# Five weight pieces instead of three converted inside the last attention steps of a decay attention followed by two MLPs

## The chip, the cores and the metric

The kernel runs on one core of a Trainium2 chip. The metric is the device time of one execution in microseconds (us). The engines of the core are TensorE (PE in the rows, with its weight loads as PEld), VectorE (DVE), ScalarE (ACT), GpSimd (POOL) and SyncE (SP, which here only issues DMAs). Each engine takes its instructions strictly in the order in which the program gives them to it, and waits at an instruction until its inputs and its output buffer are ready.

## The reference, cut to what matters

```python
# decay attention, 2 batches x 8 heads, 768 positions, head size 64, blocks of 64
for b in range(nb):
    intra = einsum('bhic,bhjc->bhij', qb, kb) * Dmask          # scores inside a block
    intra = einsum('bhij,bhjd->bhid', intra, vb)
    inter = einsum('bhid,bhde->bhie', qb * lam_pow, kv_state)  # what earlier blocks left
    out[:, :, sl] = intra + inter
    kv_state = lam_block * kv_state + einsum('bhsd,bhse->bhde', kb * rev_pow, vb)
x = out as (1536 tokens, 512)
h = x @ w_in;  x = (h * cos(h)) @ w_out         # first MLP, d_ff = 2048
h = x @ w_in2; x = (h * sigmoid(h)) @ w_out2    # second MLP, d_ff = 2048
```

The weights arrive as 64-bit floats.

## The kernel before

**Attention.** The loop over `c` from 0 to `UP` = 6 treats 128 positions (two blocks) a step, and is skewed: step `c` transposes k and q of chunk `c` on TensorE (`att_k`, `att_q`: PSUM tile `pt`, copied out by ScalarE as `kT` and `qT`, L203 and L209; `pt` has one buffer), and finishes chunk `c-1`: `att_kv` (PSUM tile `pkv`, L241), `att_state` (DVE adds it to the decayed state, L254, and POOL decays the sum, L260), `att_scores` (PSUM tile `psc`, L270, multiplied by the decay table on DVE into `at`, L274), `att_inter` (state times q, PSUM tile `pso`, L293), `att_intra` (v times `at`, added into `pso`, L308) and `att_x`. `att_x` writes the chunk of x in two float32r parts: `xhi` on ScalarE (L317) and the rest `xlo` on DVE (L318). Chunk `c` is written (c) below: `xhi`(5) is the last `xhi` of the attention.

**Weights.** A *piece* (j, p) is one tile of 128 of d_ff: p = 0 its columns of `w_in`, p = 1 its rows of `w_out`; 32 tiles make 64 pieces. `load_w` fetches a piece of 512 KB as raw 64-bit words from SyncE's queue (three buffers). `rebias_w`/`convert_w` make float32 of it: ScalarE L93, DVE L104 (`sb`) and DVE L105 (`w`). `split_w` makes two float32r parts: `hi` on ScalarE (L115) and `lo` on POOL (L116). As each piece is converted, the next load is issued (`load_next`).

**MLPs.** A second loop over `t` (96 of them) computes a tile of d_ff for 512 tokens a step: `gemm_in(t)` (12 matmuls of 128x128 by 512 into PSUM tile `h`, L347, which has two buffers; w `hi` by `xhi`, w `lo` by `xhi`, w `hi` by `xlo`, four each), the activation (ScalarE L362 and L371, DVE L363 and L377, ScalarE L379, POOL L385) and, two steps later, `gemm_out(t - 2)` (12 matmuls into `y`, L403). `h(t+1)` takes the PSUM buffer that `h(t-1)` leaves when DVE has read it at L377. h(t), y(t) and n(t) are written for these tiles of step t. Steps 0 to 3 use d_ff tiles 0 to 3, and the next eight steps the same four tiles for the other tokens; tile 4 is first wanted at t = 12.

The order is written out by hand. `first` lists the pieces converted inside the attention loop, `plan` the pieces converted at each step t of the MLP loop, and the loads go in the same order.

Of the kernel before, what the change touches and what calls it, by code (L numbers as in the profile page):

```python
# [21 lines left out]
UP = 6  # L22
# [5 lines left out]
def tile_decay_attention__two_mlps(  # L28
# [46 lines left out]
    def load_w(j, piece):  # L75
        L, f = divmod(j, FT)
        r = stage.tile([P, TB, 2], U32, tag="raw", name="raw")
        if piece == 0:
            nc.sync.dma_start(
                out=r.rearrange("p (k f) t -> p k (f t)", k=KT), in_=w_in[L][:, :, 2 * f * P:2 * (f + 1) * P]  # L80
            )
        else:
            nc.sync.dma_start(out=r.rearrange("p c t -> p (c t)"), in_=w_out[L][f * P:(f + 1) * P, :])
        raw[j, piece] = r
# [70 lines left out]
    def tables():  # L155

        step = stage.tile([P, 2, B, NP, C], F32, tag="raw", name="step")
        by_s = lamb.rearrange("p (s y) -> p y s", y=2)
        for r in range(2):
            for b in range(B):  # L160
                nc.vector.tensor_copy(step[:, r, b], by_s[:, r ^ b, :, None].to_broadcast([P, NP, C]))
        nc.vector.memset(step[:, :, :, :, 0:1], 0.0)
        scan(*(t.rearrange("p r b s i -> p (r b s i)") for t in (dm, step, diag)))
        nc.gpsimd.tensor_copy(rev, dm[:, :, :, :, C - 1].rearrange("p r b s -> p b s r"))

        first = stage.tile([P, B, NP, C], F32, tag="raw", name="first")
        nc.gpsimd.memset(first, 0.0)
        for y in range(2):
            for b in range(B):
                nc.gpsimd.tensor_copy(first[half[y], b, :, 0], by_s[half[y], y ^ b])  # L170
        for y in range(2):
            scan(*(t[half[y]].rearrange("p b s i -> p (b s i)") for t in (qp, step[:, y], first)))
# [3 lines left out]
    def load_qkv(c, parts="kqv", engine=None):  # L176
        r = slice(c * P, (c + 1) * P)
        for part in parts:
            t = ap_2.tile([P, B, H, D], F32, tag=part, name=part, bufs=3 if part == "v" else 2)
            src = [{"q": q, "k": k, "v": v}[part][b, :, r, :].rearrange("h p d -> p h d") for b in range(B)]  # L180
            eng = engine or nc.sync
            if part == "v":
                for b in range(B):
                    eng.dma_start(out=t[:, b], in_=src[b])
            else:
                eng.dma_start(out=t[:, 0], in_=src[0])
                for y in range(2):
                    eng.dma_start(out=t[:, 1, y::2, :], in_=src[1][:, 1 - y::2, :])
            qkv[c, part] = t
# [10 lines left out]
    def att_k(c, pool, tag):  # L200
        pt = transposed(c, "k", pool, tag)
        kT = ap_2.tile([P, B, NP, P], F32, tag="kT", name="kT")
        nc.scalar.copy(kT, pt)  # L203
        tr[c, "k"] = kT
# [29 lines left out]
    def att_kv(c, pool, tag):  # L234
        ps = pool.tile([P, 2, B, NP, D], F32, tag=tag, name="pkv")
        kt, vt = kd.pop(c), qkv[c, "v"]
        for b in range(B):
            for s in range(NP):
                for r in range(2):
                    for n in range(2):  # L240
                        nc.tensor.matmul(  # L241
                            ps[half[r], n, b, s, :], kt[half[n], b, 2 * s + r, :], vt[half[n], b, 2 * s + (b ^ r), :],
                            start=True, stop=True,
                        )
        pkv[c] = ps
# [185 lines left out]
    def evacuate_lo():  # L431
        if lows:
            yl, y, yh = lows.pop(0)
            nc.gpsimd.tensor_tensor(out=yl, in0=y, in1=yh, op=ALU.subtract)


    first = [(0, 0), (1, 0), (0, 1)]
    plan = {0: [(2, 0)], 1: [(1, 1), (3, 0)], 2: [(2, 1)], 3: [(3, 1)]}
    for slot, tiles in ((4, range(4, 15)), (27, range(15, 19)), (43, range(19, 27)), (67, range(27, 32))):
        for j in tiles:  # L440
            for p in range(2):
                plan[slot + 2 * (j - tiles[0]) + p] = [(j, p)]
    queue = first + [x for t in sorted(plan) for x in plan[t]]

    with tc.manual_schedule():
        nc.scalar.dma_start(out=lamb, in_=lam.partition_broadcast(P))
        load_qkv(0, "k")
        load_qkv(0, "q", nc.scalar)
        load_qkv(0, "v")
        load_qkv(1)  # L450
        zeros = stage.tile([P, TB], mybir.dt.bfloat16, tag="raw", name="zeros")
        nc.vector.memset(zeros, 0.0)
        cold = ps_o.tile([P, B, TB], F32, tag="o", name="cold")

        for _ in range(WARM):
            nc.tensor.matmul(cold[:, 0, :], zeros[:, 0:P], zeros, start=True, stop=True)
        nc.vector.memset(half_pi, math.pi / 2.0)

        nc.scalar.activation(quarter, half_pi, AF.Sin)
        nc.vector.memset(quarter, 0.25)  # L460
        nc.gpsimd.memset(ident, 0.0)
        nc.gpsimd.affine_select(
            out=ident, in_=ident, compare_op=ALU.not_equal, fill=1.0, base=0, pattern=[[-1, P]], channel_multiplier=1
        )

        diag = stage.tile([P, 2, B, NP, C], F32, tag="raw", name="diag")
        for n in range(2):
            nc.gpsimd.tensor_copy(
                diag[half[n]].rearrange("p r b s i -> p (r b s) i"), ident[half[n], None, half[n]].to_broadcast([C, B * H, C])
            )  # L470
        tables()
        loaded = 0

        def load_next():
            nonlocal loaded
            if loaded < len(queue):
                load_w(*queue[loaded])
                loaded += 1


        for c in range(UP + 1):
            if c < UP:
                att_k(c, ps_t, "t")
            if c > 0:
                att_kv(c - 1, ps_kv, "kv")
                att_state(c - 1, 0)
            if c < UP:
                att_kdec(c)
                if c + 2 < SC:
                    load_qkv(c + 2, "k")  # L490
                att_q(c, ps_t, "t")
                if c + 2 < SC:
                    load_qkv(c + 2, "qv")
            if c > 0:
                att_scores(c - 1, ps_s, "s")
                att_inter(c - 1, ps_o, "o")
            if c < UP:
                att_qdec(c)
            if c > 0:
                att_state(c - 1, 1)  # L500
                att_intra(c - 1)
                att_x(c - 1)
            if UP - 3 <= c < UP:
                load_next()
            for piece in {UP - 1: first[:1], UP: first[1:]}.get(c, ()):
                convert_w(piece)
                load_next()
                split_w(piece)
        psum_up.close()
        if UP == SC:  # L510
            att_pools.close()
        ps_h = ctx.enter_context(tc.tile_pool(name="ps_h", bufs=2, space=PSUM))
        ps_y = ctx.enter_context(tc.tile_pool(name="ps_y", bufs=6, space=PSUM))

        gpool = ctx.enter_context(tc.tile_pool(name="gpool", bufs=3))
        tpool = ctx.enter_context(tc.tile_pool(name="tpool", bufs=2))
        parts = ctx.enter_context(tc.tile_pool(name="parts", bufs=NB))
        wextra = ctx.enter_context(tc.tile_pool(name="wextra", bufs=TILES - EARLY))
        for t in range(N + 1):
            if t < N and t not in ph:  # L520
                gemm_in(t)
            if 1 <= t < N + 1:
                act_g(t - 1)
                act_glo(t - 1)
            new = t > 2 and t - 2 in starts
            if new:
                evacuate(starts[t - 2] - 1)
            evacuate_lo()
            pieces = plan.get(t, [])
            for piece in pieces:  # L530
                convert_w(piece)
                load_next()
            if t < N:
                act_a(t)
                act_b(t)
            for piece in pieces:
                split_w(piece)
            for piece in plan.get(t + 1, [])[:1]:
                rebias_w(piece)
            if new and t + 1 < N:  # L540
                gemm_in(t + 1)
            if 2 <= t < N:
                gemm_out(t - 2)

        for m in range(4):
            gemm_out(N - 2, (m,))
            gemm_out(N - 1, (m,))
        evacuate(len(runs) - 1)
# [30 lines left out]
```

## Time and profile before

| | |
|---|---|
| median of three executions | 609.42 us (608.39 to 610.33) |
| the profiled execution | 610.34 us, of which its span, first to last instruction, is 607.6 us |
| TensorE busy | 575.1 us, 95% of the span |
| VectorE, ScalarE, GpSimd busy | 323.8, 256.9, 259.3 us |
| attention ends (`xhi`(5) starts) | 73.16 us after the span's start |

Times in rows are counted from the span's start. The profiled execution lies 0.9 us above the median of the others, inside their scatter at its upper edge.

### The profile page before, as it was taken

The page shows a single profiled execution, that of the slowest core. Times are in us where ns is not written, and L with a number is a line of the kernel's source. Part 1 is how long each engine was busy: PE and PEld are TensorE (multiplying, and loading weights), DVE is VectorE, ACT ScalarE, POOL GpSimd, SP SyncE. Part 2 cuts the span into 40 slices and gives each one's busy share as a digit, 9 for nine tenths or more (in the row PEclk, how much of TensorE's full clock was granted, in tenths as well). Part 3 has the DMA queues.
Part 4 walks back from the last instruction along what each step waited for, and adds up shares of the span by engine and source line. Part 5 has one row for each costly group of instructions (what it writes and reads, how often), then busy time and mean ns, then how long its engine had stood idle before and what let it go on. Part 6 is the DMA issues. An engine that isn't in the chain of part 4 may idle for free.

```text
span 607.6 us, 9554 instructions
## 1 busy us (share of the span) xinstructions
PE 575.1 (95%) x3912; PEld 472.8 (78%) x3912; DVE 323.8 (53%) x349; ACT 256.9 (42%) x425; POOL 259.3 (43%) x201
## 2 busy tenths in 40 slices
PE   5866779999999999999999999999999999999997
PEld 2755657888888888888888888888888888888885
DVE  4354578888788877862257876611246721201212
ACT  2223355665755554563365643422433532212220
POOL 5432346555545444553266575532245541222210
PEclk9999989999999999999999999999999999999999
DMA  9986153332333322320022333300033100100101
GB/s 176 196 178 185 39 173 105 104 104 74 101 104 105 104 70 73 101 70 2 0 71 69 105 104 105 102 4 1 0 105 98 41 0 2 69 1 0 70 0 70
DMA packets 61051, 46.75 MB, mean 77 GB/s; under 512 B 38992, under 2 KB 55376, under 8 KB 61008
## 3 DMA queue, kind: packets, MB, share of 16 engines
q1 hardware_dynamic: 58768, 45.62, 26.4%
q10 hardware_dynamic: 2240, 0.53, 0.5%
q8 instruction: 30, 0.49, 0.3%
q14 instruction: 13, 0.11, 0.1%
HBM read 43.00 MB, written 3.15 MB: 76 GB/s over the span
## 4 chain that ended last, share of the span: by engine, by line
PE 91%; issue 4%; DVE 2%; ACT 1%; DMA 1%; POOL 0%; SPq 0%; DVEq 0%; ACTq 0%; POOLq 0%
PE y L403 43%; PE h L347 42%; PE pt L195 2%; PE pso L308 1%; PE pkv L241 1%; DMA k<-in_k_dram 1%; PE psc L270 1%; PE pso L293 1%; DVE w L105 1%; POOL lo L116 0%; ACT kT L203 0%; ACT xhi L317 0%; DVE sb L104 0%; ACT w L93 0%; DVE at L274 0%
## 5 line engine op out<-in xcount | busy, mean ns | idle before, releaser
L385 POOL TENSOR_TENSOR gl<-s,gh 128x512 fp32r<-128x512 f32 x95 | 133.8, 1408 | 139.1 <-ACT gh L379 124.4
L377 DVE TENSOR_TENSOR s<-h,s 128x512 f32<-128x512 f32 x96 | 66.4, 692 | 197.2 <-ACT s L373 159.2
L116 POOL TENSOR_TENSOR lo<-w,hi 128x512 fp32r<-128x512 f32 x64 | 83.5, 1305 | 156.7 <-ACT hi L115 156.7
L347 PE MATMUL h<-xhi,hi 128*128 128x512 f32 x384 | 103.5, 391 | 4.2 <-DVE s L377 3.2
L347 PE MATMUL h<-xhi,lo 128*128 128x512 f32 x384 | 103.8, 392 | 0.9 <-POOL lo L116 0.9
L347 PE MATMUL h<-xlo,hi 128*128 128x512 f32 x384 | 103.2, 391 | 0.0
L105 DVE SCALAR_TENSOR_TENSOR w<-w,sb 128x512 uint32<-128x512 uint32 x64 | 93.0, 1454 | 8.3 <-ACT w L93 1.9
L373 ACT ACTIVATE s<-h 128x512 f32<-128x512 f32 x48 | 28.8, 599 | 141.9 <-PE h L347 141.9
L347 PEld LDWEIGHTS h<-xhi,hi 128*128 128x128 f32 x384 | 71.7, 188 | 20.3 <-ACT hi L115 4.3
L347 PEld LDWEIGHTS h<-xhi,lo 128*128 128x128 f32 x384 | 72.3, 189 | 17.0 <-POOL lo L116 2.1
L347 PEld LDWEIGHTS h<-xlo,hi 128*128 128x128 f32 x384 | 72.6, 189 | 15.3
L104 DVE TENSOR_SCALAR sb<-raw 128x512 uint32<-128x512 uint32 x64 | 81.4, 1273 | 0.1
L403 PE MATMUL y<-gh,hi 128*128 128x512 f32 x192 | 74.7, 389 | 0.0
L403 PE MATMUL y<-gl,hi 128*128 128x512 f32 x192 | 74.7, 389 | 0.0
L403 PE MATMUL y<-hi,gl 128*128 128x512 f32 x192 | 74.7, 389 | 0.0
L403 PE MATMUL y<-lo,gh 128*128 128x512 f32 x192 | 74.7, 389 | 0.0
L403 PE MATMUL y<-hi,gh 128*128 128x512 f32 x192 | 74.7, 389 | 0.0
L403 PE MATMUL y<-gh,lo 128*128 128x512 f32 x192 | 74.7, 389 | 0.0
L379 ACT CAST gh<-s 128x512 fp32r<-128x512 f32 x96 | 58.9, 613 | 31.6 <-DVE s L377 23.6
L371 ACT ACTIVATE s<-s,consts 128x512 f32<-128x512 f32 x48 | 34.8, 724 | 65.4 <-DVE s L363 65.4
L362 ACT ACTIVATE n<-h,consts 128x512 int32<-128x512 f32 x48 | 33.0, 687 | 41.5 <-PE h L347 41.5
L363 DVE SCALAR_TENSOR_TENSOR s<-h,n 128x512 f32<-128x512 f32 x48 | 32.9, 685 | 31.4 <-ACT n L362 30.2
(57 smaller groups left out, 535.2 us busy)
## 6 DMA issues: line engine op xcount, KB each, us to landing
raw<-in_moe_w_in_dram SPq DMA_DIRECT2D x32, 512.0 KB, 3.8
raw<-in_moe_w_out_dram SPq DMA_DIRECT2D x32, 512.0 KB, 3.3
v<-in_v_dram SPq DMA_DIRECT2D x12, 256.0 KB, 5.0
out_dram<-part SPq DMA_DIRECT2D x12, 256.0 KB, 2.1
k<-in_k_dram SPq DMA_DIRECT2D x6, 256.0 KB, 5.2
k<-in_k_dram SPq DMA_DIRECT2D x12, 128.0 KB, 4.4
q<-in_q_dram SPq DMA_DIRECT2D x5, 256.0 KB, 4.5
q<-in_q_dram SPq DMA_DIRECT2D x10, 128.0 KB, 4.6
```

The lines of the kernel that those rows point to most:

```text
L104: nc.vector.tensor_scalar(out=sb, in0=r[:, :, 0], scalar1=2.0**-29, scalar2=7.0, op0=ALU.mult, op1=ALU.min)
L105: nc.vector.scalar_tensor_tensor(out=w, in0=w, scalar=3, in1=sb, op0=ALU.logical_shift_left, op1=ALU.bitwise_or)
L116: nc.gpsimd.tensor_tensor(out=lo, in0=w, in1=hi.bitcast(F32), op=ALU.subtract)
L347: nc.tensor.matmul(h, w[:, kt * P:(kt + 1) * P], x[:, kt, :], start=(n == 0 and kt == 0), stop=(n == 2 and kt == KT - 1),)
L362: nc.scalar.activation(n, h, AF.Identity, scale=1.0 / (2.0 * math.pi), bias=quarter)
L363: nc.vector.scalar_tensor_tensor(out=s, in0=h, scalar=1.0 / (2.0 * math.pi), in1=n, op0=ALU.mult, op1=ALU.subtract)
L371: nc.scalar.activation(s, s, AF.Sin, scale=2.0 * math.pi, bias=half_pi)
L373: nc.scalar.activation(s, ph[t], AF.Sigmoid)
L377: nc.vector.tensor_tensor(out=s, in0=ph.pop(t), in1=s, op=ALU.mult)
L379: nc.scalar.copy(gh, s)
L385: engine.tensor_tensor(out=gl, in0=act.pop(t), in1=gt[t][0].bitcast(F32), op=ALU.subtract)
L403: nc.tensor.matmul(y[m], w, x, start=(i == 0 and n == 0), stop=(i == n_tiles - 1 and n == 2))
```

## The change

Three lines of numbers change. The attention loop converts five pieces, one at the end of step c = 4, two at the end of c = 5 and two at the end of c = 6, in place of none, one and two. The MLP loop's `plan` has at t = 0, 1, 2 one piece each, and the pieces of tiles 4 to 14 start at t = 3 in place of 4. The sequence of pieces and of loads stays the same.

```diff
-    first = [(0, 0), (1, 0), (0, 1)]
-    plan = {0: [(2, 0)], 1: [(1, 1), (3, 0)], 2: [(2, 1)], 3: [(3, 1)]}
-    for slot, tiles in ((4, range(4, 15)), (27, range(15, 19)), (43, range(19, 27)), (67, range(27, 32))):
+    first = [(0, 0), (1, 0), (0, 1), (2, 0), (1, 1)]
+    plan = {0: [(3, 0)], 1: [(2, 1)], 2: [(3, 1)]}
+    for slot, tiles in ((3, range(4, 15)), (27, range(15, 19)), (43, range(19, 27)), (67, range(27, 32))):
...
-            for piece in {UP - 1: first[:1], UP: first[1:]}.get(c, ()):
+            for piece in {UP - 2: first[:1], UP - 1: first[1:3], UP: first[3:]}.get(c, ()):
                 convert_w(piece)
                 load_next()
                 split_w(piece)
```

Two places in the engines' orders matter below. The first is ScalarE between the end of step c = 4 and the end of c = 5. Before, `kT`(5) stands right behind `xhi`(3) (`xhi_722<-pso_824`):

```order
L317 CAST xhi_722<-pso_824 128x2x4x128
L203 COPY kT_910<-pt_901 128x1024
L209 COPY qT_960<-pt_951 128x1024
L317 CAST xhi_1070<-pso_997 128x2x4x128
L93 ACTIVATE w_1076<-raw_726 128x512
L115 CAST hi_1083<-w_1076 128x512
```

Now the two ScalarE instructions of piece (0, 0) stand between them:

```order
L317 CAST xhi_722<-pso_824 128x2x4x128
L93 ACTIVATE w_901<-raw_726 128x512
L115 CAST hi_908<-w_901 128x512
L203 COPY kT_921<-pt_912 128x1024
L209 COPY qT_971<-pt_962 128x1024
L317 CAST xhi_1081<-pso_1008 128x2x4x128
```

So `kT`(5) has moved behind a whole conversion, of which `hi` itself waits for DVE. The second place is DVE between `xlo`(4) at the end of c = 5 and `xlo`(5) at the end of c = 6. Before, one conversion (`sb`, `w`) stands ahead of the last state and the last `at`:

```order
L318 TENSOR_TENSOR xlo_1071<-pso_997,xhi_1070 128x2x4x128
L104 TENSOR_SCALAR sb_1078<-raw_726 128x512
L105 SCALAR_TENSOR_TENSOR w_1076<-w_1076,sb_1078 128x512
L254 TENSOR_TENSOR state_1120<-pkv_1087,sdec_1034 128x512
L274 TENSOR_TENSOR at_1155<-psc_1122,dm_91 128x1024
L318 TENSOR_TENSOR xlo_1071<-pso_1157,xhi_1070 128x2x4x128
```

Now two stand there, those of pieces (1, 0) and (0, 1):

```order
L318 TENSOR_TENSOR xlo_1082<-pso_1008,xhi_1081 128x2x4x128
L104 TENSOR_SCALAR sb_1089<-raw_899 128x512
L105 SCALAR_TENSOR_TENSOR w_1087<-w_1087,sb_1089 128x512
L104 TENSOR_SCALAR sb_1100<-raw_906 128x512
L105 SCALAR_TENSOR_TENSOR w_1098<-w_1098,sb_1100 128x512
L254 TENSOR_TENSOR state_1142<-pkv_1109,sdec_1045 128x512
L274 TENSOR_TENSOR at_1177<-psc_1144,dm_91 128x1024
L318 TENSOR_TENSOR xlo_1082<-pso_1179,xhi_1081 128x2x4x128
```

The state and `at` of chunk 5 have moved behind a second conversion. Behind `xlo`(5), the first activation's n(0) (L362 on ScalarE) has three pieces' L93 ahead of it before and after the change: (1, 0), (0, 1) and (2, 0) then, (2, 0), (1, 1) and (3, 0) now. TensorE's order does not change at all.

## Rows read from the trace of the kernel before

**Rows 1.** The page's first line.

```profile
span 607.6 us, 9554 instructions
```

**Rows 2.** Windows, one core: stretch; busy us (instructions) by engine; PEclk; DMA; GB/s.

```profile
95.00:200.00 105.00, 105.00 (x464) 86.69 (x464) 86.82 (x88) 63.69 (x111) 54.24 (x40) 1.00 0.31 96
```

**Rows 3.** Timeline: start us, us, engine, line, operation, [idle before <-releaser]; first MLP steps.

```profile
83.09 0.69 DVE L377 TENSOR_TENSOR s<-h,s 128x512 f32<-128x512 f32 x1 [0.79 <-ACT s L371]
...
83.93 1.40 PE L347 MATMUL h<-xhi,hi 128*128 128x512 f32 x4 [3.18 <-DVE s L377]
...
88.36 0.40 PE L403 MATMUL y<-gl,hi 128*128 128x512 f32 x1
...
91.11 1.07 PE L347 MATMUL h<-xhi,hi 128*128 128x512 f32 x4
...
92.88 1.20 PE L347 MATMUL h<-xhi,lo 128*128 128x512 f32 x4 [0.69 <-POOL lo L116]
```

**Rows 4.** Windows around h(2), columns as in Rows 2.

```profile
80.80:84.00 3.20, 0.07 (x1) 0.10 (x1) 2.41 (x4) 1.79 (x4) 0.71 (x2) 1.00 0.57 191
84.00:88.40 4.40, 4.40 (x13) 3.28 (x14) 4.16 (x5) 1.78 (x4) 2.35 (x2) 0.61 0.38 119
```

**Rows 5.** Timeline, end of step c = 4 to end of c = 5.

```profile
56.71 1.01 ACT L317 CAST xhi<-pso 128x1024 fp32r<-128x1024 f32 x1 [4.94 <-PE pso L308]
...
57.77 1.01 ACT L203 COPY kT<-pt 128x1024 f32<-128x1024 f32 x1
...
60.08 1.09 PE L195 MATMUL pt<-ident,q 128*128 128x128 f32 x8
...
62.34 1.22 DVE L274 TENSOR_TENSOR at<-psc,dm 128x1024 f32<-128x1024 f32 x1 [1.38 <-PE psc L270]
...
63.80 1.50 PE L308 MATMUL pso<-at,v 64*64 64x64 f32 x64
...
65.35 1.01 ACT L317 CAST xhi<-pso 128x1024 fp32r<-128x1024 f32 x1 [3.07 <-PE pso L308]
```

**Rows 6.** Timeline, end of c = 5 to end of c = 6.

```profile
67.54 0.42 DVE L104 TENSOR_SCALAR sb<-raw 128x512 uint32<-128x512 uint32 x1
...
68.67 0.68 DVE L254 TENSOR_TENSOR state<-pkv,sdec 128x512 f32<-128x512 f32 x1
68.78 0.62 ACT L115 CAST hi<-w 128x512 fp32r<-128x512 f32 x1 [1.83 <-DVE w L105]
69.27 1.22 DVE L274 TENSOR_TENSOR at<-psc,dm 128x1024 f32<-128x1024 f32 x1
...
70.36 1.16 PE L293 MATMUL pso<-qd,state 64*64 64x64 f32 x62 [1.78 <-issue]
...
71.61 1.50 PE L308 MATMUL pso<-at,v 64*64 64x64 f32 x64
...
73.16 1.01 ACT L317 CAST xhi<-pso 128x1024 fp32r<-128x1024 f32 x1 [3.76 <-PE pso L308]
```

**Rows 7.** Timeline: the second of two conversions in a row, behind `xhi`(5).

```profile
77.29 1.29 POOL L116 TENSOR_TENSOR lo<-w,hi 128x512 fp32r<-128x512 f32 x1 [6.54 <-ACT hi L115]
77.82 1.32 DVE L105 SCALAR_TENSOR_TENSOR w<-w,sb 128x512 uint32<-128x512 uint32 x1 [0.79 <-ACT w L93]
```

**Rows 8.** Timeline, step c = 2: the weight load of q's transposes.

```profile
27.21 0.85 PEld L195 LDWEIGHTS pt<-ident,q 128*128 128x128 f32 x8 [0.21 <-ACT kT L203]
```

**Rows 9.** Timeline, SyncE's queue: issue of the first two loads.

```profile
49.48 1.33 SPq L79 DMA_DIRECT2D raw<-in_moe_w_in_dram  x2
```

**Rows 10.** The tile `raw` over the whole span: its loads, issue to landing.

```profile
DMA to landing us min/median/max: 3.1/3.7/7.5
```

**Rows 11.** Timeline: 64 and 59 matmuls of the same shape, early and late.

```profile
17.35 1.99 PE L241 MATMUL pkv<-v,kd 64*64 64x64 f32 x64
...
66.49 1.09 PE L241 MATMUL pkv<-v,kd 64*64 64x64 f32 x59 [0.65 <-issue]
```

## The prediction

> **What bounds the kernel now.** I read the page's first line, then the windows, then the timeline of the one stretch where TensorE is not full. From 95 us on TensorE is busy all the time: 464 matmuls in 105 us, 0.226 us each, so 12 of them (one `gemm_in` or one `gemm_out`) take 2.72 us [rows 2]. DVE, the next engine, is at 86.8 of 105 us there. Nothing that moves a conversion by a step or two inside that stretch can gain; it can only lose if it makes TensorE wait. What can change is how late the full stretch begins, that is, the seam between attention and first MLP. In the reader's place I would look in the timeline for TensorE's idle entries there and for who ends them.
>
> There are two that count. TensorE stands 3.18 us before h(2), released by DVE's L377 [rows 3]: h has two buffers, and h(2) can't begin before the activation of t = 0 has read h(0). It stands 0.69 us in the middle of h(3) for `lo` of piece (3, 0), which POOL makes late [rows 3]. [...] h(2) begins at 83.93 and y(0) at 88.36: 4.43 us for work of 2.72 us, so the low level costs 1.7 us.
>
> In the attention, DVE leads the end: `state`(5) begins at 68.67 as soon as piece (0, 0) is done, `at`(5) at 69.27, TensorE resumes `pso` at 70.36, `at` is used at 71.61, and `xhi`(5) begins at 73.16 [rows 6].
>
> **The first added cost: `kT`(5) behind piece (0, 0).** In the kernel before, the same conversion hangs on `xhi`(4), which begins at 65.35 [rows 5]; its `hi` ends at 68.78 + 0.62 = 69.40, 4.05 us later [rows 6]. Now it hangs on `xhi`(3) at 56.71 [rows 5]. The load is no obstacle: it is issued at 49.48 [rows 9], and even the slowest landing of all, 7.5 us [rows 10], gives 57.0, before L93's turn. So `hi` ends at 56.71 + 4.05 = 60.76, and only then ScalarE copies `kT`(5), 1.01 us [rows 5], to 61.77. The transposes of q need its PSUM buffer (an earlier step shows them released by that copy [rows 8]); they began at 60.08 [rows 5] and now begin at about 61.78. That is 1.7 us. Behind them in TensorE's order stand the scores of chunk 4, then `at`(4) on DVE, `intra`(4) and `xhi`(4), each waiting for the one before. All of these were begun at 62.34, 63.80 and 65.35 [rows 5], and I move all by 1.7: `xhi`(4) to 67.05.
>
> **The second: the last state and `at` behind two conversions.** The price of two conversions in a row stands behind `xhi`(5) in the trace before: `xhi` begins at 73.16 [rows 6], the second `w` begins at 77.82 and takes 1.32 us, ending at 79.14 [rows 7], 5.98 us after `xhi`. Now the same pair hangs on `xhi`(4): it ends at 67.05 + 5.98 = 73.03. `state`(5) follows at once (73.0 in place of 68.67). From the start of `state` to the end of `at` it took 69.27 + 1.22 - 68.67 = 1.82 us [rows 6]: `at` ends at 74.8. `intra` began 0.24 us behind the end of `at`(4), 63.80 against 62.34 + 1.22 [rows 5]: it begins at 75.05. From there to `xhi`(5) it was 73.16 - 71.61 = 1.55 us [rows 6]: 76.6. So the attention ends **3.4 us later**. The last `inter` fits beside it: its 1.16 us [rows 6] start when `state` ends at 73.65.
>
> Bounds: the second `w` runs beside POOL's `lo`, which began 0.53 us earlier [rows 7]. With POOL idle, the first `sb` began at 67.54 and lasted 0.42, and `state` followed at 68.67 [rows 6], so `w` alone takes 0.7 at most; if it does so here too, the pair is 0.6 us shorter and the delay 2.8 us. Upwards, each of the three hand-overs that I carry over (to `kT`, to q's transposes, to `inter`) may cost a little over 0.1 us more than its row, 3.8 us. I take 3.4, since the rows show this very pair beside this very `lo`.
>
> **What is given back.** The weights of h(1) are now ready, but h(1) was not what the seam waited for. From `xhi`(5) to the release of h(2) the order on ScalarE and DVE is the same: two conversions, a third L93, then n(0), and L377 at last. 83.93 - 73.16 = 10.77 us, and that stays. So h(2) moves with `xhi`(5), to 87.3, and TensorE, which now runs h(0) and h(1) without a stop from 76.5 to 82, merely stands longer ahead of it, 5.3 us in place of 3.18. Behind h(2) one wait does go: `lo` of (3, 0) is now made at t = 0. h(3) took 92.88 - 91.11 = 1.77 us for its first four matmuls [rows 3] where 0.91 is the rate: **0.9 us back**. The activation of t = 1 gains too, since DVE converts one piece ahead of it in place of two, but h(3) did not wait for it. Its bounds are 0 and 1.0.
>
> Everything from tile 4 on comes one tile of d_ff earlier at the same rate, one piece a step; TensorE is full there before and should be after: nothing. The loads keep their order and stay three ahead; SyncE's queue holds nothing else at that time: nothing.
>
> **The clock.** No row shows what a longer wait does. Two places. First the attention: between the scores of chunk 5 (near 70) and `state`(5) at 73.65 TensorE now has almost 4 us with next to nothing, where it had 1.78 us [rows 6]; the 3.2 us with 0.07 busy before h(2) were followed by the low level [rows 4]. If it comes, `inter` and `intra` of chunk 5 run slowly: 64 matmuls of `pkv` took 1.99 us early in the program and 59 took 1.09 later [rows 11], so two groups of 64 cost up to 1.8 us more, of which the part behind the return of the clock is spared. Bounds 0 and 1.8; I take 0.9, nearer neither.
>
> [...]
>
> Second, h(2): it paid 1.7 us. After a wait 2.1 us longer, part of the low stretch may pass while TensorE still stands: between 1.7 back and 1 us more. I take 0.6 back.
>
> **Sum.** 3.4 - 0.9 + 0.9 - 0.6 = +2.8 us. The profiled execution, 610.34 us with its span of 607.6 [rows 1], would become 613.1; it lay 0.9 us above the median, so the median, 609.42, becomes **612.2 us**.
>
> **Rivals.**
> - *The clock stays up in the attention, and h(2) pays as before.* For it: no earlier wait of the attention, up to some 2 us, brought the low level. 3.4 - 0.9 = +2.5 at h(2)'s old price: 611.9. With 0.6 back, 611.3. I count this to the forecast's own range, 610.9 to 613.2.
> - *The clock falls twice in full.* 3.4 - 0.9 + 1.8, and up to 1 us more at h(2): +4.3 to +5.3, 613.7 to 614.7. For it: both waits are longer than the one that brought the fall before. Against it: the low stretch before lasted hardly longer than h(2)'s slow matmuls, and part of it would now fall into waits.
> - *The clock no longer falls at h(2)* (the other side: not slower). Place: h(2); price: 1.7 us back in place of 0.6; with nothing lost in the attention, 3.4 - 0.9 - 1.7 = +0.8, 610.2 us, within 0.3%. It decides if the 12 matmuls of h(2) take 2.7 us in place of 4.4. Against it: the wait that came ahead of the fall becomes longer.
> - *The change is hidden*, if DVE's pair ended before `state`(5) is wanted. TensorE resumed `pso` 1.0 us behind the end of `state` (68.67 + 0.68 against 70.36 [rows 6]), so that much is free; the pair is 4.3 us late. Were it free, only the 0.9 us back would remain: 608.5, no measurable change. I see no room for it.
>
> **Chances.** Forecast with its own range, 0.52; the clock falling twice in full, 0.22; the clock staying up at h(2), 0.18; hidden or better, 0.08. The range that leaves out 2 in 10 is 610.0 to 614.3. A measurement of this kernel tells a change from none at about 0.3%, 1.8 us, so 611.25 is the border: slower 0.70 (the forecast's case almost whole, 0.48, and 0.22), the same 0.24, faster 0.06.
>
> **What would show it.** Right: `kT`(5) begins near 60.8 behind `hi`; `state`(5) begins near 73 directly behind two conversions; `xhi`(5) near 76.6; h(1) without a wait; TensorE idle some 5 us before h(2), released by L377; no wait in h(3). Wrong: if the pair on DVE takes much less than 6 us from `xhi`(4), if h(2) is released earlier than 10.8 us behind `xhi`(5), or if a wait shows behind 97 us, where I expect none.

## The result and the profile after

Over 14 executions of each, the changed kernel takes 613.12 us (610.49 to 615.63) and the kernel before 609.36 us (606.98 to 613.69): a ratio of 1.0059, with a 95% interval of 1.0038 to 1.0081, or 3.6 us slower (2.3 to 4.9). The forecast was +2.8 us.

The profiled execution, 614.66 us, lies 1.5 us above the median of its kernel, so a second trace of the changed kernel (611.34 us) and one of the kernel before (611.63 us) were taken later; all four are used below. The first trace after: the page's first line, and the windows around h(2) with columns as in [rows 4]:

```profile
span 612.9 us, 9546 instructions
```

```profile
85.90:90.30 4.40, 0.05 (x1) 0.00 (x0) 2.83 (x5) 3.01 (x6) 1.43 (x2) 1.00 0.68 219
90.30:94.80 4.50, 4.47 (x13) 3.53 (x14) 3.61 (x4) 2.19 (x5) 2.55 (x2) 0.62 0.37 117
```

TensorE does next to nothing for 4.4 us, and then h(2) again begins at the low level (so the forecast calls the granted clock of [rows 4], 0.61): it is 0.62 here.

The timeline of the same trace, from `xhi`(3) to `xhi`(5), answers to [rows 5, 6]:

```profile
55.64 1.01 ACT L317 CAST xhi<-pso 128x1024 fp32r<-128x1024 f32 x1 [4.67 <-PE pso L308]
...
59.08 0.62 ACT L115 CAST hi<-w 128x512 fp32r<-128x512 f32 x1 [1.86 <-DVE w L105]
59.61 1.00 ACT L203 COPY kT<-pt 128x1024 f32<-128x1024 f32 x1
...
61.07 1.75 PE L241 MATMUL pkv<-v,kd 64*64 64x64 f32 x50 [4.09 <-issue]
62.76 1.97 PE L195 MATMUL pt<-ident,q 128*128 128x128 f32 x8
...
69.63 1.01 ACT L317 CAST xhi<-pso 128x1024 fp32r<-128x1024 f32 x1 [3.80 <-PE pso L308]
...
74.28 1.29 DVE L105 SCALAR_TENSOR_TENSOR w<-w,sb 128x512 uint32<-128x512 uint32 x1 [0.79 <-ACT w L93]
75.50 0.68 DVE L254 TENSOR_TENSOR state<-pkv,sdec 128x512 f32<-128x512 f32 x1
...
76.10 1.21 DVE L274 TENSOR_TENSOR at<-psc,dm 128x1024 f32<-128x1024 f32 x1
76.23 1.04 PE L293 MATMUL pso<-qd,state 64*64 64x64 f32 x56 [2.27 <-DVE state L254]
...
77.39 2.23 PE L308 MATMUL pso<-at,v 64*64 64x64 f32 x64
...
79.67 1.01 ACT L317 CAST xhi<-pso 128x1024 fp32r<-128x1024 f32 x1 [3.45 <-PE pso L308]
```

Three things are to be seen. `kT`(5) stands behind `hi`, as forecast. But TensorE did not even reach its use: it stood 4.09 us ahead of `pkv` of chunk 4 with no releaser that the profile shows ("issue"), and then worked at the low clock (0.50 granted from 61.0 to 64.8 us). And `state`(5) follows the second of two `w` at once, with TensorE waiting for it (2.27 us).

The second trace of the changed kernel has no stop of that length (1.36 us at this place), and shows the forecast's chain. The wait for `kT` that is left to TensorE is short, 0.22 us, since the 1.36 us overlap with `kT`'s lateness:

```profile
55.09 1.01 ACT L317 CAST xhi<-pso 128x1024 fp32r<-128x1024 f32 x1 [4.83 <-PE pso L308]
...
60.11 1.09 PE L195 MATMUL pt<-ident,q 128*128 128x128 f32 x8 [0.22 <-ACT kT L203]
...
63.19 1.14 PE L293 MATMUL pso<-qd,state 64*64 64x64 f32 x59 [0.79 <-issue]
...
65.98 1.01 ACT L317 CAST xhi<-pso 128x1024 fp32r<-128x1024 f32 x1 [3.67 <-PE pso L308]
...
70.63 1.29 DVE L105 SCALAR_TENSOR_TENSOR w<-w,sb 128x512 uint32<-128x512 uint32 x1 [0.79 <-ACT w L93]
71.84 0.68 DVE L254 TENSOR_TENSOR state<-pkv,sdec 128x512 f32<-128x512 f32 x1
...
75.29 1.02 ACT L317 CAST xhi<-pso 128x1024 fp32r<-128x1024 f32 x1 [2.71 <-PE pso L308]
...
85.95 2.08 PE L347 MATMUL h<-xhi,hi 128*128 128x512 f32 x4 [5.06 <-DVE s L377]
...
91.24 0.49 PE L403 MATMUL y<-gl,hi 128*128 128x512 f32 x1
...
96.81 0.39 PE L403 MATMUL y<-gl,hi 128*128 128x512 f32 x1
```

From such starts every trace can be cut into the same six legs. The table is worked out from the starts of `xhi`(3), `xhi`(4), `xhi`(5), h(2), y(0), y(1) and h(7) in the timelines (us). From h(7) to the end the spans differ by 0.3 us at most; only "three early" has 1.2 us more, behind TensorE's last matmul.

| trace | xhi(3) to (4) | xhi(4) to (5) | xhi(5) to h(2) | h(2) to y(0) | y(0) to y(1) | y(1) to h(7) | sum |
|---|---|---|---|---|---|---|---|
| before | 8.64 | 7.81 | 10.77 | 4.43 | 6.46 | 16.36 | 54.47 |
| before, second | 9.18 | 6.99 | 10.76 | 5.26 | 5.86 | 16.32 | 54.37 |
| after | 13.99 | 10.04 | 10.66 | 4.45 | 5.46 | 16.32 | 60.92 |
| after, second | 10.89 | 9.31 | 10.66 | 5.29 | 5.57 | 16.32 | 58.04 |
| `kT` first | 9.19 | 11.78 | 10.66 | 4.45 | 5.47 | 16.32 | 57.87 |
| pair behind `at` | 11.15 | 7.26 | 12.14 | 5.28 | 5.68 | 16.32 | 57.83 |
| both moved | 10.54 | 10.30 | 12.13 | 4.86 | 5.46 | 16.32 | 59.61 |
| three early | 7.36 | 10.43 | 7.11 | 3.00 | 9.12 | 16.70 | 53.72 |
| pair alone | 9.19 | 10.62 | 8.62 | 4.58 | 6.32 | 16.35 | 55.68 |
| five in gaps | 7.20 | 10.16 | 6.37 | 2.85 | 5.51 | 17.77 | 49.86 |
| five in gaps, second | 8.92 | 8.36 | 9.36 | 2.87 | 5.48 | 17.76 | 52.75 |
| filler at h(2) | 10.89 | 10.93 | 10.70 | 2.85 | 5.44 | 17.82 | 58.63 |
| filler at `inter` | 11.82 | 10.12 | 10.66 | 4.44 | 5.44 | 16.32 | 58.80 |
| both fillers | 11.91 | 9.33 | 10.71 | 2.90 | 5.44 | 17.77 | 58.06 |

The sums of the second traces differ by 3.7 us and the medians by 3.8; the sums of the first ones differ by 6.5. That 3.7 comes so close to the medians is in part luck: the two sums of the changed kernel differ by 2.9 us. A sum is also not a time: the program ahead of `xhi`(3) is the same in both kernels, yet `xhi`(3) began at 56.71 and 57.42 us before, and at 55.64 and 55.09 after, so the spans of the second traces (608.1 and 609.4 us) differ by 1.3 us only.

The column from y(1) to h(7) holds a second limit. Step 7 is the first after h(2) whose `gemm_in` stands directly behind that of the step before, with no `gemm_out` between them, so TensorE asks for h(7) one group (2.72 us) sooner than usual, and h(7) needs the PSUM buffer that L377 of t = 5 reads. First in the trace before, then in the first trace after:

```profile
110.44 0.69 DVE L377 TENSOR_TENSOR s<-h,s 128x512 f32<-128x512 f32 x1 [0.79 <-ACT s L371]
...
111.18 1.19 PE L347 MATMUL h<-xhi,hi 128*128 128x512 f32 x4
```

```profile
115.68 0.69 DVE L377 TENSOR_TENSOR s<-h,s 128x512 f32<-128x512 f32 x1 [0.79 <-ACT s L371]
...
116.56 1.09 PE L347 MATMUL h<-xhi,hi 128*128 128x512 f32 x4
```

TensorE begins h(7) 0.05 us behind the end of L377 before, and 0.19 us behind it after. From L377 of t = 0 to that of t = 5 it is 27.35 us before, where DVE converts two pieces at t = 1, and 26.09 us after, where it converts one. So however fast TensorE is, h(7) cannot begin much sooner than 27.3 us (before) or 26.1 us (after) behind h(2). If TensorE gets through its work up to h(7) within that time, what it loses on the way, by a wait or by the clock, costs nothing.

### The profile page after: what moved, and what is told of

Read it like the earlier page. It is cut to its first block, busy times and chain, and to the rows that moved or that the text cites. A ratio compares the mean times of both kernels' runs of the same rounds, so it can differ in the third digit from the quotient of the medians.

```text
span 612.9 us, 9546 instructions
## 1 busy us (share of the span) xinstructions
PE 579.4 (95%) x3912; PEld 478.6 (78%) x3912; DVE 322.4 (53%) x349; ACT 257.0 (42%) x425; POOL 258.6 (42%) x201
## 4 chain that ended last, share of the span: by engine, by line
PE 92%; issue 3%; DVE 2%; ACT 2%; DMA 1%; SPq 0%; DVEq 0%; ACTq 0%
PE y L403 43%; PE h L347 42%; PE pt L195 2%; PE pso L308 2%; PE psc L270 1%; PE pkv L241 1%; DMA k<-in_k_dram 1%; PE pso L293 1%; DVE at L274 1%; ACT xhi L317 1%; DVE w L105 0%; DVE qd L215 0%; ACT kT L203 0%; ACT w L93 0%; DVE state L254 0%
## 5 line engine op out<-in xcount | busy, mean ns | idle before, releaser
L377 DVE TENSOR_TENSOR s<-h,s 128x512 f32<-128x512 f32 x96 | 66.4, 691 | 197.1 <-ACT s L373 159.2
L362 ACT ACTIVATE n<-h,consts 128x512 int32<-128x512 f32 x48 | 33.0, 687 | 42.0 <-PE h L347 41.9
```

The source lines that it names most:

```text
L362: nc.scalar.activation(n, h, AF.Identity, scale=1.0 / (2.0 * math.pi), bias=quarter)
L377: nc.vector.tensor_tensor(out=s, in0=ph.pop(t), in1=s, op=ALU.mult)
```

## The experiments

The ratios are to the kernel before, run on the same chip between them; 1% is 6.1 us.

**`kT` first.** The conversion of (0, 0) moved behind qd(5), its `hi` behind `xhi`(4); all else as changed.

```diff
             if c < UP:
                 att_qdec(c)
+            if c == UP - 1:
+                convert_w(first[0])
+                load_next()
...
-            for piece in {UP - 2: first[:1], UP - 1: first[1:3], UP: first[3:]}.get(c, ()):
+            if c == UP - 1:
+                split_w(first[0])
+            for piece in {UP - 1: first[1:3], UP: first[3:]}.get(c, ()):
```

> The changed kernel, but the conversion of piece (0, 0) stands behind qd(5) on DVE and its hi behind xhi(4) on ScalarE, so that kT(5) is no longer behind it; all else as changed. Theory (ScalarE's order holds kT(5), then DVE's pair holds state(5)): the first 1.7 us go away, the pair stays, so the attention ends some 1.7 us before the changed kernel's, and the time is about 2 us above the kernel before (611.4 where the changed one has 613.1). Rival (what is lost is the wait without a releaser ahead of pkv of chunk 4, 4.09 us in the profile after, and the low clock behind it, which the weight loads bring about): nothing goes away, 613.

Measured: 612.71 us, ratio 1.0046 (1.0027 to 1.0065), or +2.8 us (1.6 to 4.0). The time alone doesn't decide between +2 and the rival. The first leg does: 9.19 us, as before the change (8.64 and 9.18), where the changed kernel has 10.89 at least. So what `kT`(5) added there went. The second leg took it up in this trace: the wait for `state`(5) was there as expected, and from 69.8 us on the clock was at its low level.

```profile
69.80:76.70 6.90, 5.54 (x129) 4.67 (x129) 2.71 (x3) 1.56 (x3) 1.71 (x2) 0.51 0.35 106
```

**Pair behind `at`.** The conversions of (1, 0) and (0, 1) moved behind `at`(5), their `hi` behind `xhi`(5); (0, 0) stays ahead of `kT`(5).

```diff
                 att_inter(c - 1, ps_o, "o")
+            if c == UP:
+                for piece in first[1:3]:
+                    convert_w(piece)
+                    load_next()
...
-            for piece in {UP - 2: first[:1], UP - 1: first[1:3], UP: first[3:]}.get(c, ()):
+            if c == UP:
+                for piece in first[1:3]:
+                    split_w(piece)
+            for piece in {UP - 2: first[:1], UP: first[3:]}.get(c, ()):
```

> The changed kernel, but the two conversions of pieces (1, 0) and (0, 1) stand behind at(5) on DVE and their hi behind xhi(5); (0, 0) stays where the change put it. Theory: state(5) follows xlo(4) at once, the DVE pair's 1.7 us and the long stop of TensorE before it go away, the 1.7 us of kT(5) stay: about 1 us above the kernel before (610.4). [...]

Measured: 611.78 us, ratio 1.0027 (1.0007 to 1.0048), +1.7 us (0.4 to 2.9), which holds the +1 expected. The trace: the second leg falls to 7.26 us from 9.31 and 10.04, and the wait for `kT`(5) stays alone on the first:

```profile
61.26 1.09 PE L195 MATMUL pt<-ident,q 128*128 128x128 f32 x8 [1.04 <-ACT kT L203]
...
67.40 1.01 ACT L317 CAST xhi<-pso 128x1024 fp32r<-128x1024 f32 x1 [3.94 <-PE pso L308]
...
74.66 1.01 ACT L317 CAST xhi<-pso 128x1024 fp32r<-128x1024 f32 x1 [5.09 <-PE pso L308]
```

Not expected: the third leg grew by 1.5 us to 12.14, because the moved `hi`s and POOL's two `lo`s now stand behind `xhi`(5), in front of the next conversions: `sb` and `w` of the next piece took 1.01 and 1.59 us beside those `lo`s, against 0.41 and 0.69 us in the second trace after.

**Both moved.** Both edits together, on the changed kernel.

> Both moves at once: three pieces are converted ahead of xhi(5), none in the way of kT(5) or state(5), and two behind xhi(5) ahead of n(0) as in the changed kernel. Theory: xhi(5) begins where it did before (73.2 us, give or take the instruction gaps), h(2) is still released 10.8 us behind it, the wait in h(3) is gone: 0.9 us below the kernel before, 608.5. Rival (h(1)'s ready weights are worth something to the seam): 2 us or more below.

Measured: 612.84 us, ratio 1.0038 (1.0016 to 1.0059), +2.3 us (1.0 to 3.6): a miss by 3 us, and not to the rival's side. The trace names three costs that the expectation left out. The conversion behind qd(5) stands ahead of `state`, which empties the one PSUM buffer of `pkv`, so TensorE waited for it ahead of `pkv` of chunk 5:

```profile
67.14 1.34 PE L241 MATMUL pkv<-v,kd 64*64 64x64 f32 x62 [1.57 <-DVE state L254]
```

Behind it came a stop of 2.33 us without a releaser and a stretch of 0.50 granted clock from 72.0 to 75.3, and the third leg is 12.13 again.

**Three early.** The kernel before with its three early pieces at the places of that run and its own MLP plan, so that one L93 alone is left between `xhi`(5) and n(0).

```diff
+            if c == UP:
+                for piece in first[1:3]:
+                    convert_w(piece)
+                    load_next()
...
+            if c == UP - 1:
+                convert_w(first[0])
+                load_next()
...
-            for piece in {UP - 1: first[:1], UP: first[1:]}.get(c, ()):
+            if c == UP - 1:
+                split_w(first[0])
+            if c == UP:
+                for piece in first[1:3]:
+                    split_w(piece)
+            for piece in ():
```

> The kernel before in its first three pieces and its plan of the MLP steps, but these three are converted at the places of the run with both moves, all ahead of xhi(5); so between xhi(5) and n(0) only one L93 is left. Theory (the seam waits for n(0), which stands behind two conversions in both kernels): h(2) is released some 5 us sooner behind xhi(5), TensorE's stop of 3.2 us before h(2) shrinks to under 1 us and the low clock of h(2) goes with it: 4 to 5.5 us below the kernel before, 604 to 605.5. Rival (h(2) waits for its own weights just as well): at most 1 us below, 608.5.

Measured: 609.17 us, ratio 0.9981 (0.9959 to 1.0004), -1.2 us (-2.5 to +0.2): much less than expected, and no clear gain. The mechanism is there: h(2) is released 7.11 us behind `xhi`(5) in place of 10.77, with 1.29 us of waiting, and h(2) takes 3.00 us. But the fifth leg, y(0) to y(1), grew to 9.12: with h(2) early, h(3)'s weights, converted second at t = 1, are late, and TensorE waits twice in h(3), the second time ending in slow matmuls (groups of four in 1.66 and 1.91 us, 1.07 in h(4)). The second leg grew as well, to 10.43 us, with TensorE at a granted clock of 0.50 from 70.9 to 74.3 us.

```profile
81.90 1.17 PE L347 MATMUL h<-xhi,hi 128*128 128x512 f32 x4 [1.29 <-DVE s L377]
88.58 1.20 PE L347 MATMUL h<-xhi,hi 128*128 128x512 f32 x4 [0.80 <-ACT hi L115]
90.85 1.66 PE L347 MATMUL h<-xhi,lo 128*128 128x512 f32 x4 [1.07 <-POOL lo L116]
```

**Pair alone.** One part of the change alone, on the kernel before.

```diff
-            for piece in {UP - 1: first[:1], UP: first[1:]}.get(c, ()):
+            for piece in {UP - 1: first[:2], UP: first[2:]}.get(c, ()):
```

> The kernel before with one piece moved: (1, 0) is converted at the end of c = 5 behind (0, 0) in place of c = 6; nothing at c = 4, the MLP steps' plan as before. Theory: state(5) stands behind two conversions, so xhi(5) begins 9.6 to 10 us behind xhi(4) in place of 7.8, about 2 us later; but only one conversion is left ahead of n(0), so h(2) is released some 8.2 us behind xhi(5) in place of 10.7: the two cancel, within 1 us of the kernel before. Rival (the seam waits for h(2)'s own weights): xhi(5) later, h(2) still 10.7 us behind it: 2 us above.

Measured: 611.64 us, ratio 1.0044 (1.0023 to 1.0065), +2.7 us (1.4 to 4.0), more than expected. The legs decide against the rival: h(2) is released 8.62 us behind `xhi`(5) (8.2 expected, 10.7 by the rival). The second leg is 10.62, with the clock at 0.51 from 71.8 to 75.3 us, and in its trace 1.2 us of the sum are left. So the 2.2 us that n(0) gains are eaten by the second leg, which is 2.8 us longer by the pair and the clock together; the rest of the +2.7 this trace doesn't show.

**Second traces of the changed kernel and of the kernel before**, one execution each.

> The changed kernel once more, for a second trace. If the 4.09 us wait ahead of pkv of chunk 4 belongs to the change, it stands here too. If it is chance, xhi(4) begins 10.3 us behind xhi(3) (its 8.6 us of before and the 1.7 us of kT(5)) in place of the 14.0 us of the first trace, and the 10 us from xhi(4) to xhi(5) stay.

> The kernel before once more, for a second trace. If the low clock inside the attention belongs to the changed orders, none stands here before 80 us, as in the first trace; if the attention stands at the edge of it anyhow, a low stretch shows here too. From xhi(3) to xhi(5) 16.5 us without one, up to 2 us more with one.

The 4.09 us stop is not in the second trace after (1.36 us there); the first leg is 10.89 and the second 9.31, against 10.3 and 10 expected. In the second trace before, a low stretch stands inside the attention:

```profile
56.00:60.00 4.00, 3.74 (x64) 3.03 (x54) 1.23 (x1) 1.66 (x2) 0.19 (x1) 0.57 0.65 227
84.30:89.60 5.30, 5.25 (x12) 4.14 (x13) 4.63 (x5) 2.32 (x5) 2.47 (x2) 0.50 0.33 106
```

So the low clock in the attention needs no change of order, and h(2) can stand at the low level throughout in the kernel before too (second row: 0.50, with 5.26 us to y(0)). From `xhi`(3) to `xhi`(5) this trace took 16.17 us, less than the 16.5 expected without a low stretch, so no price of it shows there. The first trace before was the untypical one: it is the only one of the fourteen without a low stretch between 28 and 62 us (granted clock 1.00 there; eight transposes take 1.09 us in it and 1.97 in the low stretch of the second trace before), and its mean granted clock, 0.997, is above all the 0.977 to 0.994 of the later executions of the same kernel.

**Filler at h(2).** The changed kernel with 18 extra matmuls between h(1) and h(2).

```diff
-        if i == 0:
+        if i == 0 and r not in py:
...
+            if t == 2:
+                py[0] = [ps_y.tile([P, TB], F32, tag="y", name="y") for _ in range(4)]
+                for _ in range(18):
+                    nc.tensor.matmul(py[0][0], wt[0, 0][0][:, 0:P], xt[0][0][:, 0, :], start=True, stop=True)
```

> The changed kernel with 18 matmuls more between h(1) and h(2), each 128x512 into a y tile that y(0) starts afresh; their sums are used nowhere. They fill TensorE's wait for L377 with 18 x 0.226 = 4.1 us of work. Theory (of the seam's loss, what stands at h(2) beside the wait itself is the low clock: 4.4 to 5.3 us from h(2) to y(0) in place of 2.7): h(2) begins as before 10.7 us behind xhi(5) and takes 2.7 us; 1.7 to 2.5 us below the changed kernel, so some 1.5 us above the kernel before. Rival (h(2) is slow for another reason, its weights or its x): as the changed kernel, 3.7 us above.

**Filler at `inter`.** The changed kernel with 20 extra transposes in the wait for `state`(5).

```diff
+                if c == UP:
+                    fill = ps_t.tile([P, B, NP, P], F32, tag="t", name="fill")
+                    for _ in range(20):
+                        nc.tensor.transpose(fill[:, 0, 0, :], ident, ident)
```

> The changed kernel with 20 transposes more (of the identity, into a PSUM buffer that nothing reads) between the scores and inter of chunk 5, 0.13 us each, 2.5 us in the wait for state(5). Theory of the prediction (the wait for state(5) brings the low clock onto inter and intra, 0.9 us): no low stretch begins between xhi(4) and xhi(5), 9.3 us from the one to the other in every trace; about 0.5 to 1 us below the changed kernel. [...]

**Both fillers.**

> Both fillers. If the low clock is all that the seam loses beyond the engines' orders, the sum is 3.4 - 0.9 = 2.5 us for the orders less 1.7 us that h(2) no longer pays: within 1 us of the kernel before. Rival: 2.5 us or more above it.

Measured: 613.04 us, ratio 1.0067 (1.0044 to 1.0091), for the first; 612.76 us, 1.0057 (1.0040 to 1.0074), for the second; 611.30 us, 1.0034 (1.0020 to 1.0048), for both: +4.1, +3.5 and +2.1 us. At h(2) the filler does what it should; with the engine busy until 0.47 us before h(2), the clock stays at 1.00 and h(2) takes 2.85 us:

```profile
88.50 1.20 PE L347 MATMUL h<-xhi,hi 128*128 128x512 f32 x4 [0.47 <-DVE s L377]
...
91.35 0.39 PE L403 MATMUL y<-gl,hi 128*128 128x512 f32 x1
```

```profile
72.00:78.80 6.80, 5.10 (x123) 4.43 (x124) 2.55 (x3) 1.62 (x3) 1.55 (x2) 0.50 0.34 99
88.50:91.30 2.80, 2.80 (x12) 2.35 (x13) 2.70 (x2) 1.39 (x3) 2.53 (x2) 1.00 0.15 19
```

Yet the median did not move. The first of these windows shows one loss of this trace: the clock was low for `inter` and `intra` (second leg 10.93). The other is at h(7), where TensorE lost again what h(2) had gained, waiting for L377 of t = 5:

```profile
113.86 0.69 DVE L377 TENSOR_TENSOR s<-h,s 128x512 f32<-128x512 f32 x1 [0.79 <-ACT s L371]
...
114.61 1.20 PE L347 MATMUL h<-xhi,hi 128*128 128x512 f32 x4 [1.34 <-DVE s L377]
```

From h(2) to h(7) it is 26.11 us with the filler, against 26.23 and 27.18 in the two traces after. So the low clock, which made h(2) itself 1.6 and 2.4 us longer there, had cost only 0.1 and 1.1 us by h(7). The expectation "1.7 to 2.5 us below the changed kernel" failed on this, though h(2) became as fast as expected, so not for the rival's reason.

With both fillers the clock is at 1.00 from 72 us on, the second leg 9.33 and h(2) 2.90; h(7) waits 1.30 us for L377, and the sum is that of the second trace after (58.06 against 58.04). The time is 1.5 us below that of the changed kernel by the ratios (1.0059 against 1.0034; the intervals overlap). The filler at `inter` alone gained nothing, and its second leg, 10.12 us at a granted clock of 1.00, was longer than the 9.31 of the second trace after. So the filler at h(2) buys nothing in these traces, because DVE holds h(7); whether both together gain anything is not clear of the noise, and the expectation "within 1 us of the kernel before" for both failed by 1 us.

**Five in the gaps.** The five pieces of the change, each placed where DVE and ScalarE stand idle in the trace before, on the kernel before; run twice.

```diff
-    first = [(0, 0), (1, 0), (0, 1)]
-    plan = {0: [(2, 0)], 1: [(1, 1), (3, 0)], 2: [(2, 1)], 3: [(3, 1)]}
+    first = [(0, 0), (1, 0), (0, 1), (2, 0), (1, 1)]
+    plan = {1: [(3, 0)], 2: [(2, 1)], 3: [(3, 1)]}
...
                 att_k(c, ps_t, "t")
+            if c == UP - 1:
+                split_w(first[0])
...
                 att_intra(c - 1)
+                for piece in {UP - 2: first[:1], UP - 1: first[1:2], UP: first[2:4]}.get(c, ()):
+                    convert_w(piece)
+                    load_next()
+                if c == UP:
+                    split_w(first[2])
                 att_x(c - 1)
+            if c == UP - 1:
+                split_w(first[1])
-            if UP - 3 <= c < UP:
+            if UP - 4 <= c < UP - 1 and loaded < 4:
                 load_next()
-            for piece in {UP - 1: first[:1], UP: first[1:]}.get(c, ()):
-                convert_w(piece)
-                load_next()
-                split_w(piece)
+        split_w(first[3])
+        convert_w(first[4])
+        load_next()
...
                 act_b(t)
+            if t == 0:
+                split_w(first[4])
```

> Five pieces converted around the attention's last steps as in the change, but each in a stretch in which DVE and ScalarE stand idle in the trace of before: (0, 0) between state(4) and xlo(3) with its hi behind kT(5), (1, 0) between state(4)'s successor and xlo(4), (0, 1) and (2, 0) between at(5) and xlo(5), (1, 1) behind xlo(5) with its hi behind the Sin of t = 0; piece (3, 0) is converted at t = 1, the pieces of tile 4 on start at t = 4 as before. The first load is issued a step earlier. Theory (the seam costs what stands in the engines' orders ahead of kT(5), state(5) and n(0)): the attention ends as in the kernel before, h(2) is released some 7 us behind xhi(5) in place of 10.7, the wait in h(3) goes: 4 to 6 us below the kernel before. [...]

> The run with five pieces in the gaps once more, on another chip or at another time: 3.5 to 5 us below the kernel before, h(2) again 6.4 us behind xhi(5) and no wait over 0.5 us behind it. If the first result was chance, less than 2 us below.

Measured: 605.25 us, ratio 0.9938 (0.9916 to 0.9960), and 605.77 us, ratio 0.9943 (0.9924 to 0.9963): 3.8 and 3.5 us below the kernel before. The first is just short of the 4 to 6 us expected, the second at the edge of its 3.5 to 5; both are below all other versions.

```profile
75.19 1.01 ACT L317 CAST xhi<-pso 128x1024 fp32r<-128x1024 f32 x1 [3.62 <-PE pso L308]
...
81.56 1.20 PE L347 MATMUL h<-xhi,hi 128*128 128x512 f32 x4 [0.27 <-DVE s L377]
```

In the first trace h(2) is released 6.37 us behind `xhi`(5), after a wait of 0.27 us in place of 3.18, and none over 0.15 us follows up to h(7). There both traces wait 1.28 us for L377, as with the filler at h(2); that is a miss of the second expectation, which had no wait over 0.5 us:

```profile
107.69 1.19 PE L347 MATMUL h<-xhi,hi 128*128 128x512 f32 x4 [1.28 <-DVE s L377]
```

The second trace misses the 6.4 us: it has 9.36, since h(0) itself was late.

```profile
76.38 0.86 PE L347 MATMUL h<-xhi,hi 128*128 128x512 f32 x3 [1.80 <-issue]
77.08 1.81 PE L347 MATMUL h<-xhi,lo 128*128 128x512 f32 x4
...
80.63 0.69 ACT L362 ACTIVATE n<-h,consts 128x512 int32<-128x512 f32 x1 [4.32 <-PE h L347]
...
83.58 1.20 PE L347 MATMUL h<-xhi,hi 128*128 128x512 f32 x4 [0.17 <-DVE s L377]
```

TensorE stopped for 1.80 us behind the first matmul of h(0) and then worked slowly (four matmuls in 1.81 us, 1.08 at the same place in the trace before); here ScalarE waits for TensorE (4.32 us ahead of n(0)), no longer the reverse, and TensorE's wait before h(2) is 0.17 us. In both traces h(2) takes 2.85 to 2.87 us and the fifth leg 5.5. The attention itself is slower in both traces (the first two legs are 17.4 and 17.3 us, before 16.5 and 16.2). So what pays in these traces is the way from `xhi`(5) to L377, which the change left as it was, and DVE's one conversion fewer between h(2) and h(7): 26.1 us there, before 27.3 and 27.4. The change has the second of these too. No run parts the two.

## Why the prediction was right

Right were the direction, the range (613.1 us measured, 610.9 to 613.2 forecast) and the chain up to h(2). Behind h(2) one term came out right for a reason that the forecast had set aside, and one was mis-sized. Step by step:

- *`kT`(5) behind (0, 0), 1.7 us.* `hi` ends 4.06 us behind `xhi`(3) in both traces after (59.08 + 0.62 - 55.64 in the first), forecast 4.05. The transposes of q begin 5.02 us behind `xhi`(3) in the second trace after, 1.65 us later than in [rows 5]. The first leg grows by 1.7 us between the second traces, and goes back to 9.19 when this part alone is undone. That the leg comes out at the forecast's 1.7 is in part luck: the transposes stood at 3.91 us in the second trace before, which makes 1.1, and the other 0.6 is a stop ahead of `inter`(4) of 0.79 us in place of 0.19.
- *`state`(5) behind two conversions, 1.7 us.* The pair ends 5.94 us behind `xhi`(4) (70.63 + 1.29 - 65.98), forecast 5.98. The second leg is 9.31, forecast 9.55. But between the second traces it grows by 2.3 us, since the leg of before is 6.99 there: the 7.81 of [rows 5, 6] held a stop of TensorE of 1.78 us, which was 1.23 in the second trace. In that trace it was this stop, and not DVE, that led the end of the attention: `state` was done at 69.35 us, and TensorE resumed at 70.36. The pair was taken at the right length and compared with one long row.
- *10.77 us from `xhi`(5) to h(2), unchanged.* 10.66 in both traces after, 10.66 to 10.71 wherever this order stood, and 8.62, 7.11 and 6.37 when conversions were taken out of it. This was the point on which the sign hung.
- *0.9 us back in h(3).* The fifth leg, y(0) to y(1), is 5.46 and 5.57: the wait is gone. It is 1.0 less than in the first trace before, 0.3 less than in the second. But the wait for `lo` was not what this time hung on. In the first trace before DVE released h(7) at 111.13 us and TensorE began it at 111.18, so without the wait in h(3) it would have stood just as much longer before h(7). What gives time back is DVE's one conversion fewer at t = 1, of which the forecast said that h(3) did not wait for it: L377 of t = 5 comes 27.35 us behind that of t = 0 before and 26.09 after, and h(2) to h(7) falls from 27.25 to 26.23 us (first traces) and from 27.44 to 27.18 (second). That the size came out near is luck.
- *The clock.* This is the term that was mis-sized: 0.6 us back at h(2) did not come. h(2) to y(0) takes 4.45 and 5.29 after, 4.43 and 5.26 before. Without it the forecast's sum is 3.4 us, beside 3.6 measured. The 1.7 us that the forecast let h(2) pay were also not a price that the run pays in full, since h(7) waits for DVE; the rival in which all 1.7 come back could not have come true in these traces, for with the clock up (the filler at h(2)) 1.5 of the 1.6 us were lost again by h(7), 1.34 of them in the wait before it. The 0.9 us in the attention is supported only in part: in three of the traces with the change's pair the low level stood on `inter` or `intra` (granted clock 0.54 from 77.4 to 79.7 us in the first after, 0.51 in `kT` first, 0.50 in the filler at h(2)), in the second after it did not (`intra` in 1.50 us, as before the change); and it comes in kernels without the change's orders. Its bound of 1.8 us rested on [rows 11], where the granted clock is 1.00 in both rows, so they show no price of the low level; `intra` of chunk 5 took 2.23 us at 0.54 in the first trace after, 0.7 us more than before.

Between the second traces the terms are +1.7, +2.3, -0.1, 0.0 and -0.3, together 3.7, with nothing from y(1) to h(7). What the forecast did not have at all is the 4.09 us stop of the first trace after. It is not in the second, and so it isn't needed for the result; whether the changed orders make long stops there more frequent is open: it was 4.09, 1.36, 0.55, 1.89, 1.94 and 2.99 us in the six traces with a conversion ahead of `kT`(5), and none to 1.62 us in the eight without one, too few to tell.

## What to carry to other kernels

Moving work earlier gains only if it leaves the chain that ends last; here five conversions in place of three passed ahead of the seam, and still two of them stood between the last x and the first activation, so nothing came sooner and what they displaced came later. On engines that run in order, ask of each moved instruction what stands behind it and whether it waits for another engine itself: `hi`, waiting for DVE, held `kT`, which held a PSUM buffer, which held TensorE (for 1.04 us in the trace of the pair behind `at`). A wait or a slow stretch has a price only if no other limit stands behind it: look for the next point where another engine holds this one, as DVE did at h(7), before a saving is counted. Where a stage of 40 us has waits that come and go, take two traces of the kernel before, since a single row of it may hold a chance stop.

## What the runs showed of the hardware

- TensorE's stops without a releaser in the attention come at even distances in its program: the trace before resumes from such stops at 59.13, 62.57 and 66.49 us [rows 11], and in between stand 127 and 126 matmuls, each with its weight load (50 + 8 + 64 + 5, and 59 + 64 + 3). It resumes again at 70.36 and 74.23 us, so the resumes are 3.4 to 3.9 us apart. TensorE's timeline between the first two:

```profile
59.13 1.02 PE L241 MATMUL pkv<-v,kd 64*64 64x64 f32 x50 [1.07 <-issue]
...
61.11 1.16 PE L270 MATMUL psc<-qT,kT 64*64 64x64 f32 x64
62.09 0.29 PE L293 MATMUL pso<-qd,state 64*64 64x64 f32 x5
62.57 1.15 PE L293 MATMUL pso<-qd,state 64*64 64x64 f32 x59 [0.19 <-issue]
```

  In the traces these stops are 0.2 to 4.1 us long. What TensorE waits for in them, no trace and no run shows.
- A wait of TensorE of 3.0 to 6.1 us before h(2) was followed by the low level in all nine traces with one (granted clock 0.50 to 0.64 over h(2)). Over h(2) it was 1.00 in the two traces with five pieces in the gaps, behind waits of 0.27 and 0.17 us, and in the two with the filler at h(2), 4.24 us of matmuls in the first, behind 0.47 and 1.02 us. In the attention, where TensorE was busy 22.6 of the 34 us from 28 to 62 us in the first trace before, the granted clock was 1.00 over that stretch there and 0.57 from 56 to 60 us in the second execution of the same kernel.
